# Dummy matmuls and two short reads in the first microseconds of a fused linear-attention and MLP kernel

## The chip, the cores and the metric

The kernel runs on one core of one Trainium2 chip. The time is the device time of one execution in microseconds; the one used core is also the slowest core. Profiles come from the hardware profiler, taken in one execution of the program; their times are counted from the first instruction of the program's span.

## What is computed

The first part is a linear attention with 8 batches, 8 heads, 576 positions and 64 features per head. Its feature map is a ReLU whose output is weighted by a cosine and by a sine of the position. The second part is an MLP over the resulting 4608 rows of 512 features, with a hidden width of 2048 and a Swish whose slope `beta` differs per hidden feature.

```python
def phi(x, c, s):
    r = np.maximum(x, 0.0)
    return np.concatenate([r * c, r * s], axis=-1)
k_p, q_p = phi(k, cos_w, sin_w), phi(q, cos_w, sin_w)
kv = np.einsum('bhsf,bhsd->bhfd', k_p, v)
z = np.sum(k_p, axis=2)
num = np.einsum('bhsf,bhfd->bhsd', q_p, kv)
den = np.einsum('bhsf,bhf->bhs', q_p, z)[..., None] + 1e-06
x = (num / den), heads side by side            # 4608 x 512
h = x @ w_in                                   # 512 x 2048
g = h / (1 + exp(-beta * h))
out = g @ w_out                                # 2048 x 512
```

## The kernel before

The 4608 rows are worked in nine chunks of 512 rows (`TCH`). Each chunk goes through `x @ w_in` into PSUM, a Swish on ScalarE, and `g @ w_out`; from the second chunk on, TensorE uses sums of blocks of the operands (tiles `S1` to `S4`, `T1` to `T4`), made on VectorE, to save matmuls. The attention of batch b runs ahead of the chunk that needs it. The order of the work is written out by hand: every engine executes its instructions in the order of the code, and only semaphores hold an engine back.

What matters here is the opening, before the first chunk. The steps, with the lines of the profile:

- SyncE issues the loads of batch 0 in the order q (two halves), v first half, k first half, v second half, k second half (two pieces), and then `w_in`, all with `load_raw` (L79) and `load_w` (L103). They lie in one hardware queue. ScalarE issues a small load of `beta` (L131).
- GpSimd makes the position numbers `it9` (L142) and two identity matrices: `identf` (64 by 64, float32, L162) and `ident` (128 by 128, bfloat16, L164). It multiplies part of v by the sine (`v_scale`, L209) once v is there.
- VectorE clears `zeros`, which is a part of `S1` (L145 and L160), and makes `tan9` from sine and cosine (L175, L176). Later it copies the tangent table from PSUM (L694), takes the ReLU of q (`q_relu`, L193), multiplies the transposed q by the tangent (`tan_mul`, L223), multiplies v by the cosine (`v_scale`, L209) and takes the ReLU of a part of k (`k_relu`, L193).
- TensorE first executes `warm_pe(58, 48)` (L685): 58 matmuls of zeros by zeros with 48 columns, whose result nobody reads. Then it transposes the tangent (L689) and `beta` (L692), executes 6 dummies of 128 columns and 9 of 48 (L700, L701), transposes q with `ident` in two groups of nine (`q_turn_pe`, L235) with one dummy of 512 columns between them (L704), executes `warm_long(2)` (float32 dummies on raw q, L679), and goes on with `kv_mm` (L276) and `num_mm` (L297). All bfloat16 dummies stand at L675 in the profile.
- The division (L308, L312, L319), the transposes of x (L356) and the first matmuls of chunk 0 (L386) follow.

`S2` is a constant tile of bfloat16, 128 partitions by 8 by 256. In the kernel before, it is written for the first time by the sums of the second chunk (L406).

The 58 copies out of `o_sb` that GpSimd issues (L537) go through its own, software-made queue.

Of the kernel before, what the change touches and what calls it, by code (L numbers as in the profile page):

```python
# [10 lines left out]
FP32 = mybir.dt.float32  # L11
# [5 lines left out]
P = 128  # L17
NQ = 9
# [4 lines left out]
def kernel(  # L23
# [14 lines left out]
    nc = tc.nc  # L38
# [21 lines left out]
    part = ctx.enter_context(tc.tile_pool(name="part", bufs=2))  # L60
# [29 lines left out]
    S1, S2, S3, S4 = (const.tile([P, JT // 2, TCH // 2], BF16, name=f"S{i}") for i in (1, 2, 3, 4))  # L90
# [69 lines left out]
    nc.vector.memset(zeros[:, P:512], 0.0)  # L160
    identf = const.tile([HP, HP], FP32, name="identf")
    make_identity(nc, identf)  # L162
    ident = const.tile([P, P], BF16, name="ident")
    make_identity(nc, ident)  # L164

# [29 lines left out]
    def q_relu(b, jp, eng="dve", n0=0, n1=NQ):  # L195
        return relu(qb[:, jp, n0:n1].rearrange("q n (j d) -> q j n d", j=2),
                    raw_tile(b, "q")[:, 2 * jp : 2 * jp + 2, n0:n1], eng)
# [29 lines left out]
    def q_turn_pe(b, jp, bank, hold=False):  # L227

        parts = ((0, 0, 5), (1, 5, NQ))
        v2 = []  # L230
        for i, n0, n1 in parts:
            t = ps[:, bank + i].bitcast(BF16)[:, 0 : (n1 - n0) * P].rearrange("q (n c) -> q n c", c=P)
            v2.append(t)
            for n in range(n0, n1):
                nc.tensor.matmul(t[:, n - n0, :], lhsT=qb[:, jp, n, :], rhs=ident,  # L235
                                 is_transpose=True, start=(n == n0), stop=(n == n1 - 1))
        def take(e, i):
            _, n0, n1 = parts[i]
            if e == "act":
                nc.scalar.copy(qts[b % 2][:, jp, n0:n1], v2[i])  # L240
            else:
                tan_mul(nc.vector, qs_first[:, jp, n0:n1], v2[i], n0, n1)

        if hold:
            return take
        for e, i in (("act", 0), ("dve", 1), ("act", 1), ("dve", 0)):
            take(e, i)
# [425 lines left out]
    def warm_pe(count, w=512, bank=1):  # L673
        for i in range(count):
            nc.tensor.matmul(ps[:, bank, 0:w], lhsT=zeros[:, 0:P], rhs=zeros[:, 0:w], start=True, stop=True)  # L675
# [6 lines left out]
    beta = const.tile([P, JT], FP32, name="beta")  # L682
    rbeta = const.tile([P, JT], FP32, name="rbeta")

    warm_pe(58, 48)  # L685

    for bank, n0, n1 in ((6, 0, 5), (7, 5, NQ)):
        for n in range(n0, n1):
# [8 lines left out]
    nc.vector.tensor_copy(ps[:, 0, 0:NQ], cos9)  # L697
    nc.vector.tensor_copy(ps[:, 0, 16 : 16 + NQ], sin9)
    q_relu(0, 1)
    warm_pe(6, 128, bank=2)  # L700
    warm_pe(9, 48, bank=2)  # L701
    q_turn_pe(0, 0, 4)
    nc.vector.reciprocal(rbeta, beta)
    warm_pe(1)  # L704
# [387 lines left out]
```

## Time and profile before

| What | us |
| --- | --- |
| Three runs: median (lowest to highest) | 273.6 (273.07 to 273.94) |
| Span of the profiled execution, first to last instruction | 272.7 |
| TensorE busy in the span | 265.3 (97%) |
| VectorE busy | 224.0 (82%) |
| ScalarE busy | 188.4 (69%) |
| GpSimd busy | 68.3 (25%) |

No time of its own beside the span is given for the profiled execution. The runs are 0.4 to 1.2 us above its span, the median 0.9 us: what lies around the span, and the differences between executions.

In the rows of the profile, "PE" is TensorE's matmul, "PEld" its weight load, "DVE" VectorE, "ACT" ScalarE, "POOL" GpSimd and "SP" SyncE; a "q" behind a name is the engine's instruction queue, which issues DMAs. [...] A row of the windows gives busy time of each engine in a stretch, the clock that TensorE was granted, the share of time that the 16 DMA engines were busy, and the bytes that they moved per second.

### The profile page before, as it was taken

To read this page: it belongs to the slowest core of one execution; us is meant where nothing else is said; L and a number is where in the kernel's file an instruction comes from. 1 tells how busy PE (TensorE), PEld (TensorE's weight loads), DVE (VectorE), ACT (ScalarE), POOL (GpSimd) and SP (SyncE) were. 2 spreads that over 40 slices of the span, in tenths; PEclk is the share of its full clock that TensorE was granted. 3 is DMA by queue.
4 is the path that set the end of the run, shared out by engine and by line. 5 is a ranking of instruction groups with operands and counts; after the bars stand their busy time and mean duration, and the time that the engine had idled before them with its cause. 6 is when DMAs were issued, how large, how long until landed. Compare 5 with 4: busy or idle time off the path is not lost.

```text
span 272.7 us, 8970 instructions
## 1 busy us (share of the span) xinstructions
PE 265.3 (97%) x3712; PEld 206.8 (76%) x3712; DVE 224.0 (82%) x596; ACT 188.4 (69%) x384; POOL 68.3 (25%) x89
## 2 busy tenths in 40 slices
PE   8899999999899999999999999999999999999994
PEld 8554455455784588888888888888888888888883
DVE  5989969499989889789989997899589768757852
ACT  4778777796419656899489966996696179428920
POOL 1444000510078000660085009300840060000001
PEclk9999999999999999999999999999999999999999
DMA  6999999999969999994589439943600570015005
GB/s 237 374 395 383 392 390 319 379 201 336 284 130 311 240 348 226 240 313 103 147 216 370 92 58 223 332 71 62 181 2 2 61 185 1 2 27 130 0 2 155
DMA packets 50681, 54.00 MB, mean 198 GB/s; under 512 B 31232, under 2 KB 31760, under 8 KB 50640
## 3 DMA queue, kind: packets, MB, share of 16 engines
q1 hardware_dynamic: 47504, 45.55, 59.1%
q0 software_dynamic: 2784, 7.61, 9.6%
q8 instruction: 29, 0.48, 0.7%
q10 hardware_dynamic: 352, 0.27, 0.4%
q14 instruction: 12, 0.10, 0.1%
HBM read 36.71 MB, written 9.44 MB: 169 GB/s over the span
## 4 chain that ended last, share of the span: by engine, by line
PE 85%; DVE 9%; DMA 3%; SPq 1%; issue 1%; ACT 1%; DVEq 0%
PE ps L621 32%; PE ps L511 27%; PE ps L386 10%; PE ps L544 5%; PE ps L563 4%; PE ps L297 3%; DMA raw_v<-in_v_dram 3%; PE ps L276 3%; DVE vb L219 1%; DVE xs L319 1%; DVE qs L223 1%; SPq L79 1%; DVE S L406 1%; DVE rk L193 1%; DVE qb L193 0%
## 5 line engine op out<-in xcount | busy, mean ns | idle before, releaser
L537 POOL DMA_DIRECT2D out_dram<-o_sb x58 | 33.9, 591 | 147.3 <-ACT o_sb L658 86.3
L420 ACT ACTIVATE g_t<-ps,beta 128x512 bf16<-128x512 f32 x96 | 60.3, 702 | 1.4 <-PE ps L511 1.3
L621 PEld LDWEIGHTS <-S 128*128 128x128 bf16 x448 | 43.4, 98 | 5.2
L511 PE MATMUL ps<-w_stage 128*128 128x256 bf16 x288 | 46.6, 272 | 0.1
L386 PE MATMUL ps<-xt,win 128*128 128x512 bf16 (+1 forms) x196 | 42.8, 375 | 0.1
L511 PEld LDWEIGHTS <-w_stage 128*128 128x128 bf16 x384 | 37.3, 98 | 5.1 <-issue 0.2
L487 DVE TENSOR_TENSOR ps<-ps,p 128x256 f32<-128x256 f32 x74 | 30.5, 428 | 8.6 <-PE ps L511 3.0
L394 ACT ACTIVATE g_t<-ps,beta 128x512 bf16<-128x512 f32 x48 | 32.3, 688 | 7.2 <-PE ps L386 7.1
L621 PEld LDWEIGHTS <-g_t 128*128 128x128 bf16 x336 | 32.3, 98 | 4.5 <-ACT g_t L420 0.4
L386 PEld LDWEIGHTS <-win 128*128 128x128 bf16 x196 | 18.7, 98 | 21.1 <-issue 0.5
L511 PE MATMUL ps<-xt,win 128*128 128x256 bf16 x192 | 32.9, 273 | 0.0
L511 PEld LDWEIGHTS <-win 128*128 128x128 bf16 x288 | 28.0, 98 | 3.4
L621 PE MATMUL ps<-wout,g_t 128*128 128x256 bf16 x224 | 28.9, 273 | 0.0
L406 DVE TENSOR_TENSOR S<-g_t 128x512 bf16<-128x512 bf16 (+1 forms) x66 | 25.7, 418 | 3.3 <-ACT g_t L420 1.7
L480 ACT COPY ps<-ps 128x256 f32<-128x256 f32 x62 | 22.6, 383 | 7.5 <-PE ps L621 4.0
L217 ACT ACTIVATE vb<-raw_v,sin 128x256 bf16<-128x256 f32 (+1 forms) x58 | 26.0, 503 | 1.5 <-DMA raw_v<-in_v_dram 1.5
L621 PE MATMUL ps<-T,S 128*128 128x256 bf16 x224 | 26.6, 273 | 0.0
L621 PE MATMUL ps<-wout,S 128*128 128x256 bf16 x224 | 26.4, 273 | 0.0
L319 DVE TENSOR_TENSOR xs<-ps,rden 128x768 bf16<-128x768 f32 (+4 forms) x26 | 22.8, 884 | 0.9 <-DVE rden L312 0.2
L223 POOL TENSOR_TENSOR qs<-qt,tanr 128x1152 bf16<-128x1152 bf16 x6 | 14.3, 2387 | 27.4 <-PE ps L563 21.0
L658 ACT COPY o_sb<-ps 128x512 f32<-128x512 f32 x11 | 6.3, 587 | 20.1 <-PE ps L621 20.1
L487 DVE TENSOR_TENSOR ps<-ps,u 128x256 f32<-128x256 f32 x36 | 15.3, 427 | 5.3 <-PE ps L511 3.3
(112 smaller groups left out, 414.7 us busy)
## 6 DMA issues: line engine op xcount, KB each, us to landing
raw_v<-in_v_dram SPq DMA_DIRECT2D x7, 1152.0 KB, 9.7
raw_k<-in_k_dram SPq DMA_DIRECT2D x7, 1152.0 KB, 9.5
raw_q<-in_q_dram SPq DMA_DIRECT2D x7, 1152.0 KB, 7.4
out_dram<-o_sb POOLq DMA_DIRECT2D x58, 128.0 KB, 4.5
w_stage<-in_moe_w_in_dram SPq DMA_DIRECT2D x3, 1024.0 KB, 12.8
w_stage<-in_moe_w_out_dram SPq DMA_DIRECT2D x2, 1024.0 KB, 7.9
w_stage<-in_moe_w_out_dram SPq DMA_DIRECT2D x4, 512.0 KB, 11.9
out_dram<-o_sb SPq DMA_DIRECT2D x10, 128.0 KB, 2.4
```

The lines of the kernel that those rows point to most:

```text
L217: got = nc.scalar.activation(o, a, AF.Copy, scale=t[:, n : n + 1])
L223: return eng.tensor_tensor(dst.rearrange("q n (g p) -> q n g p", g=2), src.rearrange("q n (g p) -> q n g p", g=2), tanr[:, n0:n1].unsqueez ...
L319: nc.vector.tensor_tensor(o.rearrange("q j n s d -> q j (n s) d"), nv[:, :, a:z, :, 0:D].rearrange("q j n s d -> q j (n s) d"), rden[:, :, ...
L386: nc.tensor.matmul(ps[:, h_bank(c, jt), i * 64 : (i + w) * 64], lhsT=win[jt // 4][:, mi, (jt % 4) * P : (jt % 4 + 1) * P], rhs=xt[:, i : i ...
L394: return nc.scalar.activation(gs[c, jt // 4][:, jt % 4], ps[:, h_bank(c, jt)], AF.Silu, scale=beta[:, jt : jt + 1])
L406: return nc.vector.tensor_tensor(o, l, r, op=op)
L420: return nc.scalar.activation(gs[c, jt // 4][:, jt % 4], bank, AF.Silu, scale=beta[:, jt : jt + 1])
L480: return nc.scalar.copy(at("a", 0), at("b", 0))
L487: nc.vector.tensor_tensor(dst, at("b", 0), st["p5"], op=ALU.add)
L511: nc.tensor.matmul(dst, lhsT=l[:, g], rhs=r[:, :, g * HP : (g + 1) * HP], start=start and g == 0, stop=g == 1, skip_group_check=True)
L537: (eng or own).dma_start(out=out_v[bb, n][:, m0:m1], in_=o_sb[hf * HP : (hf + 1) * HP, m0:m1])
L621: nc.tensor.matmul(dst, lhsT=l(i), rhs=r[:, i], start=start and i == 0, stop=i == order[-1], skip_group_check=True)
```

## The change

In the opening, `warm_pe(58, 48)` becomes `warm_pe(5)`, that is 5 dummies of 512 columns; the 6 of 128 columns and 9 of 48 become 2 of 512 and 2 of 48. The other dummies stay. Counted over TensorE's instructions, 64 matmuls and 64 weight loads are gone, of some 7,400 instructions.

Between the making of `identf` and of `ident`, GpSimd issues two DMAs. Each reads from batch 0 of v, or of k, 16 floats (64 bytes) at each of 64 places: 16 destination partitions (every eighth of the partition order that `load_raw` uses) by 4 groups of heads. They land in `S2`, where nothing reads them. The real loads of v and k are unchanged, as are the orders on VectorE, ScalarE and SyncE.

```diff
     identf = const.tile([HP, HP], FP32, name="identf")
     make_identity(nc, identf)
+
+    def early_rows(src, part):
+        rows = src[0].rearrange("(j g) (p n) d -> (g p) j (n d)", g=2, n=NQ)[0:P:8, :, 0:16]
+        nc.gpsimd.dma_start(out=part, in_=rows)
+
+    first = S2.rearrange("q i t -> q (i t)").bitcast(FP32)[0:P:8].rearrange("q (i j e) -> q i j e", j=4, e=16)
+    early_rows(v, first[:, 0])
+    early_rows(k, first[:, 1])
     ident = const.tile([P, P], BF16, name="ident")
     make_identity(nc, ident)
...
-    warm_pe(58, 48)
+    warm_pe(5)
...
     q_relu(0, 1)
-    warm_pe(6, 128, bank=2)
-    warm_pe(9, 48, bank=2)
+    warm_pe(2, bank=2)
+    warm_pe(2, 48, bank=2)
     q_turn_pe(0, 0, 4)
```

## The prediction

> **What bounds the kernel now.** I read the busy times first, then the chain of waits over the first 20 us, VectorE's timeline and the windows there, and last the durations of equal matmuls before and after 9 us.
>
> ```profile
> PE 265.3 (97%) x3712; PEld 206.8 (76%) x3712; DVE 224.0 (82%) x596; ACT 188.4 (69%) x384; POOL 68.3 (25%) x89
> 18.60:30.00 11.40, 11.35 (x74) 5.58 (x75) 10.34 (x23) 9.51 (x15) 2.94 (x5) 1.00 1.04 387
> ```
>
> TensorE fills the span, and from 18.6 us on it is busy without a break (11.35 of 11.40 us). So a microsecond won or lost by 18.6 us is won or lost at the end. The change acts before that, where TensorE's 97% says nothing, since its work there is largely dummies.
>
> ```profile
> 3.16 9.06 DMA raw_v<-in_v_dram
> 12.25 0.92 DVE vb L209
> 18.65 0.40 PE ps L356 x4
> ```
>
> The chain there starts with the second half of v, issued at 3.16 and landed at 12.22, and then runs through VectorE (12.25 to 18.60) until TensorE's transposes of x at 18.65. The chain names a DMA, but the reader should ask how long VectorE would have been busy without it:
>
> ```profile
> 5.13 0.75 DVE L193 TENSOR_SCALAR qb<-raw_q 128x1152 bf16<-128x1152 f32 x1
> 6.32 0.76 DVE L193 TENSOR_SCALAR qb<-raw_q 128x1152 bf16<-128x1152 f32 x1
> 9.16 1.34 DVE L209 TENSOR_TENSOR vb<-raw_v,ps 128x1152 bf16<-128x1152 f32 x1
> 10.46 0.86 DVE L193 TENSOR_SCALAR rk<-raw_k 128x512 bf16<-128x512 f32 x1
> 11.24 0.81 DVE L223 TENSOR_TENSOR qs<-ps,tanr 128x640 bf16<-128x640 bf16 x1
> 12.25 1.35 DVE L209 TENSOR_TENSOR vb<-raw_v,ps 128x1152 bf16<-128x1152 f32 x1 [0.19 <-DMA raw_v<-in_v_dram]
> ```
>
> VectorE waits for v only 0.19 us (12.05 to 12.25). Before that, its only idle stretch from 5.13 us is about 0.07 us ahead of the ReLU of q's second half, which landed at 6.30. From 6.32 its instructions touch each other. The data arrive only just in time, but VectorE's own work is as long.
>
> ```profile
> 4.00:5.00 1.00, 1.00 (x11) 0.84 (x10) 0.64 (x2) 0.58 (x2) 0.00 (x0) 1.00 1.04 406
> 5.00:6.00 1.00, 1.00 (x16) 1.00 (x17) 1.00 (x4) 0.00 (x0) 0.00 (x0) 1.00 0.95 311
> 6.00:7.00 1.00, 1.00 (x13) 0.92 (x10) 0.89 (x3) 0.31 (x1) 0.00 (x0) 1.00 1.02 350
> 7.00:8.00 1.00, 1.00 (x9) 0.80 (x8) 0.96 (x3) 0.54 (x2) 0.00 (x0) 1.00 1.00 350
> 8.00:9.00 1.00, 1.00 (x6) 0.71 (x4) 1.00 (x3) 1.00 (x2) 0.00 (x0) 1.00 1.03 373
> ```
>
> The last two numbers are the busy share of the DMA engines and GB/s. When v and k begin to move, at 5 us, the engines stay busy but move less: against 406 GB/s, the four stretches lack 95, 56, 56 and 33 KB, 240 KB in all, or 0.59 us of the full rate. The packet records show why: most packets of 2304 bytes take 0.093 us, but the first of v, at 5.12 us, took 0.96 us, and some 70 up to 9.7 us took 0.13 to 0.75 us.
>
> ```profile
> L235 PE MATMUL ps<-ident,qb x18: 289/314/314, 5.9 to 8.2; 128*128 128x128 bf16 x18
> L356 PE MATMUL ps<-ident,xs x16: 219/219/229, 15.2 to 18.8; 128*128 128x128 bf16 x16
> L679 PE MATMUL ps<-raw_q,S x6: 592/592/1017, 8.3 to 13.6; 128*128 128x512 f32 x6
> ```
>
> Equal transposes took 314 ns up to 8.2 us and 219 ns after 15 us (minimum/median/maximum stand in the rows), and the float32 dummy 1017 ns at 8.26 and 592 ns from 9.1 on. TensorE thus ran slowly until 9.0 us, where the clock's record begins with 1.0; the windows' 1.00 before that is only its absence. It had been busy since 0.99 us.
>
> **The change part by part.** *First dummies.* Before: 58 in 2.50 us (0.99 to 3.49), starts 0.040 us apart. After: 5 of 512 columns. The one such dummy at 6.88 us let its successor start at 7.30, so 0.43 us each, 2.13 us; they need all of `zeros`, cleared at 1.16, and end near 3.35. The tangent's transposes wait for `tan9`, ready at 3.42. They start at 3.56 as before: cost 0. The margin is 0.1 to 0.2 us; without it VectorE's table copies at 4.36 and all behind them come later by what is missing, less the 0.07 us of idle ahead of 6.32.
>
> *Second dummies.* Before 15 from 4.90 to 5.94; after 2 x 0.43 + 2 x 0.04 = 0.93 us, to 5.83. The transposes of q wait for the ReLU, which ends at 5.88. Cost 0, hidden by the ReLU.
>
> *Clock.* The trace has the old pattern open the clock at 9.0 us and cannot show the new one. One bound: it opens several microseconds earlier. Then 18 transposes go at less than 0.107 us each (5.94 to 6.88 and 7.30 to 8.26), but VectorE, busy from 6.32 on, would gain at most the 0.04 us ahead of 7.12. Other bound: it opens after the first 36 `kv_mm`. The four float32 dummies then stand 0.85 us apart (8.26 to 9.11) and not 0.43, end at 11.7, and `kv_mm` (11.25, 0.70 us long) ends near 12.9 in place of 11.95; ScalarE's copy of kv (12.01) comes 0.9 us later, with its four v products, its ReLU of k (to 14.43) and the second `kv_mm` behind it, which had 0.14 us of room: +0.75 us. I take 0, the value nearest to the row: more columns per weight load is hardly less activity.
>
> [...]
>
> *GpSimd.* Two issues ahead of `ident`. GpSimd's issues of stores have a mean of 0.591 us: 1.2 us, so `ident` is ready at 3.4 in place of 2.16; first use 5.94. Cost 0 with 2.5 us of cover; without it, each microsecond would delay q's transposes. GpSimd's next work is v at 9.14. Its first stores come at 50.81, and no order there changes. `S2` is next written at 67.9, far behind the landing.
>
> *Early reads.* Issued at 1.6 and 2.2 us. Nearest rows for landing: 2.6 us for the 8 KB of `beta`, 4.5 us for 128 KB stores of GpSimd. So v's places are touched by 4.2 to 6.1 us and k's 0.6 us later; v's real packets start at 5.0, k's near 6.5. Gain, if the touches take all the slow packets away: v's second half lands 0.59 us earlier. VectorE can use only 0.19 of it, and 0.04 elsewhere: -0.23 us. If they take nothing away: 0. Cost: 128 short packets on 16 engines, 8 each. `beta`'s 512-byte packets took 0.025 us, so 0.2 us; this lies in front of q's second half, whose landing VectorE follows within 0.02 us. The other bound is a slow first packet per engine there (second rival). I take the gain at 0.23, since a third of the slow packets gone already gives the 0.19, and the cost at 0.05, between 0 and 0.2: q's half lands with its slowest engine, and most of the others, done up to some 0.8 us earlier in the packet records, have room for eight short packets.
>
> *Sum.* 0 + 0 + 0 - 0.23 + 0.05, about -0.2 us: span 272.5, and with the 0.9 us that the median lies above the span, 273.4. I say 273.3, as some executions may also open the clock earlier.
>
> **The rivals.** *The clock was the matter in other executions* (faster). The runs spread over 0.87 us, which is about the +0.75 us of a late opening. If the executions at 273.60 and 273.94 paid for it and wide dummies always open the clock in time, the new time is the lowest run less the sum: 273.07 - 0.2 to 0.4, 272.7. For it: clock open only after 8 us of dummies, so it is near the point (10.4 us, where the float32 dummies end) from which it costs. Against: only one execution is traced, and its span is itself within 0.4 us of the lowest run.
>
> *Slow first packets moved in front of q* (slower). If the places are slow because they are new to an engine, the early read pays this itself, at 3 to 5 us, on the engines that carry q. With the 0.96 us packet there, q's second half lands at 7.2, all of VectorE comes 0.9 us later, the wait of 0.19 vanishes, and 0.2 us of short packets join: +0.9 us, 274.5. It decides once q is more than 0.2 us late. For it: VectorE's 0.02 us margin at 6.32. Against: 64-byte reads can wait beside q's packets.
>
> [...]
>
> *The reads change nothing* (they come too late, or the slow packets have another cause): 273.6.
>
> **How the numbers follow.** Forecast 0.46 at 273.3, clock 0.32 at 272.7, moved packets 0.14 at 274.5, nothing 0.08 at 273.6. A difference under 0.3% (0.82 us, about the spread of the runs) can't be told from none: faster means under 272.78, slower over 274.42. Faster: most of the second and a tail of the first, 0.34; slower: the third, 0.14; same 0.52. The range goes from 272.4 (full gain and early clock) to 274.4 (most of the moved packets).
>
> **What would show it.** In the new profile: the tangent's transposes still at 3.56 and q's at 5.94; `ident` made by 4 us; windows from 5 to 9 us near 400 GB/s if the touches work; q's ReLU still at 6.32, else the second rival; float32 dummies all at 592 ns if the clock opened earlier; VectorE without the 0.19 us wait and L356 at 18.45. The forecast falls if L356 moves by more than 0.5 us, or if it stays and the end moves.

## The result, and the profile after

The changed kernel is slower: 278.7 us, median of six runs (277.03 to 279.55), against 273.85 us (273.07 to 274.86) for the kernel before in six. The ratio is 1.0162, with a 95% interval of 1.0141 to 1.0184. The traced execution after took 277.81 us with a span of 276.0, so 1.8 us lie around the span. By that, the traced execution of before (span 272.7) was one of about 274.5 us, 0.65 above the median. The two traces therefore show 3.3 of the 4.85 us between the medians. One run of the reads alone (277.71 us) and one of 16 dummies more (278.66 us), in the experiments below, were slow at a lower clock (0.994 and 0.988), are untraced, and stay out of the medians and ratios.

The totals hardly help. These lines of the page after are the engines' busy times, the granted clock in 40 slices of 6.9 us, and the queue that carries instructions.

```profile
PE 265.9 (96%) x3648; PEld 204.6 (74%) x3648; DVE 223.8 (81%) x596; ACT 188.2 (68%) x384; POOL 68.4 (25%) x91
PEclk9989999999999999999999999999999999999999
q8 instruction: 28, 0.46, 0.7%
```

TensorE is as busy as before, and the 64 matmuls and 64 weight loads are gone. One slice of the clock shows an 8. The last row stood at `q8 instruction: 29, 0.48, 0.7%` in the page of before, a row that is easy to pass over at 0.7%. The packet records say what it is: 29 packets of 16 KB before, 28 after.

VectorE's timeline after (start, duration, engine, line, operation; in brackets the idle time ahead of it and what ended it) shows where its part of the forecast went.

```profile
6.23 0.76 DVE L201 TENSOR_SCALAR qb<-raw_q 128x1152 bf16<-128x1152 f32 x1
...
11.66 1.35 DVE L217 TENSOR_TENSOR vb<-raw_v,ps 128x1152 bf16<-128x1152 f32 x1
...
15.07 1.17 DVE L115 CAST win<-w_stage 64x512 bf16<-64x512 f32 x2
18.90 0.17 DVE L316 TENSOR_TENSOR den<-ps,eps 128x14 f32<-128x14 f32 x1 [2.65 <-PE ps L305]
```

q's ReLU is at 6.23 (6.32 before), and v's second half at 11.66 (12.25 before) without a wait for a DMA. The opening did gain. Then VectorE sits idle for 2.65 us, waiting for TensorE. So the next view is the chain of waits between 10 and 30 us (start, duration, what).

```profile
15.10 0.40 PE ps L364 x4
15.50 0.41 PE ps L305 x30
15.90 2.42 issue
18.32 0.65 PE ps L305 x30
18.97 2.63 PE ps L394 x6
```

The transposes of x (L364, L356 before) start their second group at 15.10; before, it was 15.68. Then, between two halves of a row of `num_mm` (L305), comes 2.42 us of "issue": the profile knows of nothing that TensorE waited for. TensorE's own timeline has the place.

```profile
15.67 0.21 PE L305 MATMUL ps<-kv,qs 64*64 64x65 bf16 x4
15.70 0.20 PE L305 MATMUL ps<-kv,qt 64*64 64x65 bf16 x2
18.32 0.26 PE L305 MATMUL ps<-kv,qt 64*64 64x65 bf16 x2 [2.42 <-issue]
...
105.41 0.83 PE L629 MATMUL ps<-T,S 128*128 128x256 bf16 x6 [0.99 <-issue]
```

A group of four equal matmuls is torn in two: two run at 15.70, the other two 2.6 us later, with the same operands long at hand. (Rows of neighbouring matmuls overlap: the first two above start 0.03 us apart and show 0.21 and 0.20 us.) In the trace of before the same group is whole:

```profile
16.29 0.20 PE L297 MATMUL ps<-kv,qt 64*64 64x65 bf16 x4
```

The hole ends with no semaphore, so the description of the kernel, by which only semaphores hold an engine back, leaves something out. A second such hole stands at 104.42. The windows after (busy time of PE, PEld, DVE, ACT, POOL with their counts, granted clock, DMA share, GB/s) show what surrounds the first.

```profile
15.00:18.30 3.30, 0.86 (x40) 0.59 (x38) 1.18 (x3) 1.67 (x4) 2.82 (x5) 0.96 1.05 395
18.30:22.00 3.70, 3.68 (x45) 1.94 (x46) 2.96 (x10) 0.66 (x3) 0.00 (x1) 0.58 1.04 386
```

The DMA engines are full (1.05) through the hole. Near its end the granted clock falls: the clock's record has 0.5 from 18.02 to 21.43. The first six matmuls of `x @ w_in` took 2.63 us there (18.97 in the chain above); in the trace of before the same six are the row `16.81 1.46 PE L386 MATMUL ps<-xt,win 128*128 128x512 bf16 x6`. That is 1.17 us more.

**The account of the traces.** Opening earlier: -0.58 us. First hole: +2.42. Half clock on six matmuls: +1.17. Second hole: +0.99. One wait of before at 69.19, of 0.96 us and on semaphores, is absent: -0.96. Sum +3.04 of the 3.3; some 0.3 us I did not trace.

**What the hole is.** Queue 8 carried 29 packets of 16 KB for TensorE's 7,424 matmuls and weight loads, about 256 instructions to a packet. The division is only rough (28 packets for 7,296 after); the places of the holes are exact. I number TensorE's records, that is its matmuls, weight loads and waits, in order of their start. In the changed kernel and the experiments 17 holes of 0.5 us or more behind 13 us have no wait. Ten of them end at record 450, or 450 and a multiple of 256 (706, 1986, 2754, 3010, 3778, 5314); the other seven, all behind number 1200, end two to four numbers short of such a place, and I take it that those traces lack some records. The first packet after began at 15.91, and TensorE went on at 18.32, 2.4 us later. My reading: instructions come in blocks by DMA, beside the data (the page gives queue 8 0.7% of the 16 engines' span), and the block that TensorE needed at record 450 was late, so that it had no instructions. Before, 128 more instructions stood ahead, so the same boundary lay among other work. The experiments test that.

### The profile page after: what moved, and what is told of

It reads as the page before. It is cut to its first block, busy times and chain, and to the rows that moved or that the text cites. A ratio compares the mean times of both kernels' runs of the same rounds, so it can differ in the third digit from the quotient of the medians.

```text
span 276.0 us, 8847 instructions
## 1 busy us (share of the span) xinstructions
PE 265.9 (96%) x3648; PEld 204.6 (74%) x3648; DVE 223.8 (81%) x596; ACT 188.2 (68%) x384; POOL 68.4 (25%) x91
## 4 chain that ended last, share of the span: by engine, by line
PE 88%; DVE 9%; issue 2%; ACT 1%; DVEq 0%
PE ps L629 31%; PE ps L519 27%; PE ps L394 11%; PE ps L552 5%; PE ps L305 4%; PE ps L284 3%; PE ps L571 3%; DVE qs L231 2%; DVE S L414 1%; DVE vb L227 1%; PE ps L683 1%; DVE xs L327 1%; PE ps L243 1%; PE ps L364 1%; DVE qb L201 0%
## 5 line engine op out<-in xcount | busy, mean ns | idle before, releaser
L545 POOL DMA_DIRECT2D out_dram<-o_sb x58 | 32.6, 570 | 151.9 <-ACT o_sb L666 86.4
L394 PE MATMUL ps<-xt,win 128*128 128x512 bf16 (+1 forms) x196 | 44.3, 383 | 0.0
L227 DVE TENSOR_SCALAR vb<-raw_v,cos 128x256 bf16<-128x256 f32 x63 | 20.0, 367 | 0.0
```

The lines of the kernel that those rows point to most:

```text
L227: got = nc.vector.tensor_scalar(o, a, scalar1=t[:, n : n + 1], scalar2=None, op0=ALU.mult)
L394: nc.tensor.matmul(ps[:, h_bank(c, jt), i * 64 : (i + w) * 64], lhsT=win[jt // 4][:, mi, (jt % 4) * P : (jt % 4 + 1) * P], rhs=xt[:, i : i ...
L545: (eng or own).dma_start(out=out_v[bb, n][:, m0:m1], in_=o_sb[hf * HP : (hf + 1) * HP, m0:m1])
```

## The experiments

The ratios are to the kernel before, run on the same chip, with 95% intervals.

**Only the dummies, only the reads.** The first takes the change's three edits of `warm_pe` without the DMAs, the second the two DMAs without those edits.

```diff
-    warm_pe(58, 48)
+    warm_pe(5)
...
-    warm_pe(6, 128, bank=2)
-    warm_pe(9, 48, bank=2)
+    warm_pe(2, bank=2)
+    warm_pe(2, 48, bank=2)
```

> The nine wide dummies in place of 73 narrow ones, without the two early reads. Theory (TensorE's instructions come in blocks over the DMA engines; 128 fewer instructions ahead of the dense small matmuls let TensorE use up its block before the next one has come): a hole of about 2.4 us in TensorE inside the second half of the num matmuls (L297) near 16 us, that waits for no semaphore, the first 16 KB instruction packet after 15 us, and a time of 277 to 279.5 us. Rival 1 (the early reads cause the loss): no hole, 273 to 274.2 us. Rival 2 (wide dummies upset the clock gate, and the hole is a consequence): clock lost before any hole.

> The kernel before with the two early reads added, all 73 narrow dummies kept. Theory: no hole near 16 us, first 16 KB instruction packet near 10 us as before, 273.2 to 274.2 us (ratio 0.997 to 1.002). Rival 1 (the reads cause the loss): 277 us or more.

The dummies alone: 278.72 us (four runs), ratio 1.0174 (1.0121 to 1.0227). The reads alone: 273.84 us (nine runs), 1.0003 (0.9977 to 1.0029). So the whole loss is the dummies'. TensorE's timeline with the dummies alone has the hole at the same record:

```profile
15.97 0.20 PE L297 MATMUL ps<-kv,qt 64*64 64x65 bf16 x2
18.92 0.22 PE L297 MATMUL ps<-kv,qt 64*64 64x65 bf16 x2 [2.75 <-issue]
```

A later block is late in this trace too, with a hole of 1.13 us that ends at 106.88. The four runs also bound what the clock adds: the two at a mean clock of 1.0 took 277.42 and 278.04, the two at 0.992 and 0.994 took 279.4 and 280.15, about 2 us more.

**The count restored.** Wide dummies and reads as in the change, but 66 dummies of 16 columns added and two wide ones taken away, so that TensorE's count is that of before.

```diff
-    warm_pe(5)
+    warm_pe(3)
+    warm_pe(32, 16)
...
     warm_long(2)
+    warm_pe(34, 16)
```

> The changed kernel with TensorE's instruction count restored: 3 wide dummies and 32 of 16 columns at the start, 34 of 16 columns after the float32 dummies, so that as many instructions as before precede the kv matmuls. Reads kept. Theory: the hole near 16 us is gone, 273 to 274.5 us. Rivals (reads, or wide dummies and the clock): still 277 us or more, or a clock lost near 16 to 18 us.

Measured 273.69 us (ten runs), 0.9993 (0.9974 to 1.0011). The timeline at the same matmuls, no group torn:

```profile
16.34 0.23 PE L305 MATMUL ps<-kv,qt 64*64 64x65 bf16 x4
...
16.81 0.21 PE L305 MATMUL ps<-kv,qt 64*64 64x65 bf16 x4
16.84 0.21 PE L305 MATMUL ps<-kv,qs 64*64 64x65 bf16 x4
```

Sixty-four more matmuls that compute nothing bring 5 us back. The kind of dummy isn't the matter; their number is. Record 450 now lies in the second `kv_mm`, and a break of 0.18 us stands exactly there in the records (15.10 to 15.28, merged in the view): the block came just in time.

**64 dummies more.** If only the place in blocks of 256 matters, 128 instructions more should hurt like 128 fewer.

```diff
-    warm_pe(58, 48)
+    warm_pe(90, 24)
...
     warm_long(2)
+    warm_pe(32, 16)
```

> The kernel before with 64 dummies more (90 of 24 columns in place of 58 of 48; 32 of 16 columns after the float32 dummies), no early reads, no wide dummies: the count is shifted by +128 instructions, which is the same place in a block of 256 as -128. Theory: a hole inside the second half of the num matmuls as in the changed kernel, 1.5 to 3 us, and 276 to 280 us. Rivals (fewer instructions as such, the wide dummies, the reads): no hole, 273.5 to 275 us, the rise only from a later start of the kv matmuls.

Measured 279.61 us (four runs), 1.0208 (1.017 to 1.0247), with the hole one block later in the count (at record 706) but at the same instructions:

```profile
16.08 0.20 PE L297 MATMUL ps<-kv,qt 64*64 64x65 bf16 x2
18.57 0.22 PE L297 MATMUL ps<-kv,qt 64*64 64x65 bf16 x2 [2.30 <-issue]
```

Two later holes stand in this trace as well, 0.93 us to 105.46 and 1.25 us to 131.03. Together with the last one, this experiment rules out that too little or too weak dummy work is the cause.

**The opening's DMA load taken away.** The changed kernel, with all loads of `w_in` held until ScalarE's second copy of kv; one run.

```diff
-            nc.sync.dma_start(out=st[:, a : a + step], in_=w_in_v[:, a : a + step, i * 512 : (i + 1) * 512])
+            got = nc.sync.dma_start(out=st[:, a : a + step], in_=w_in_v[:, a : a + step, i * 512 : (i + 1) * 512])
+            if behind is not None:
+                after(got, behind, "w_in behind kv")
...
-    load_w("in", 0, 2)
...
-    for i in range(1, 4):
-        load_w("in", i)
...
-    kv_take((1,), 6, eng="act")
+    held = kv_take((1,), 6, eng="act")
+    load_w("in", 0, 2, held)
+    for i in range(1, 4):
+        load_w("in", i, 4, held)
```

> The changed kernel with all loads of w_in held until ScalarE has copied the second kv (about 15 us), so that the DMA engines have little to carry between 13 and 15.5 us; TensorE's instructions are the same. The h matmuls then wait for w_in, and the time is longer for that (about 277 to 282 us). Theory with the DMA load as the cause of the late block: the first 16 KB packet runs by 14 us and there is no hole without a semaphore in the second num matmuls. Rival (a block always takes about 6 us): the packet near 16 us and the hole of about 2.4 us stay.

It took 282.7 us, a little over the 277 to 282 expected. TensorE now waits 4.05 us for `w_in`, and two later blocks are late (1.71 us to 54.39, 1.38 us to 110.29); that time says nothing of the hole in the opening. The two DMA views from 12 us on (queue, packets, MB, share of the 16 engines), first of the changed kernel, 12 to 15.5 us, then of this one:

```profile
q1 hardware_dynamic: 670, 1.30, 101.9%
```

```profile
q1 hardware_dynamic: 46, 0.09, 6.5%
q8 instruction: 1, 0.02, 2.1%
```

With the engines full, no block came by 15.5. With the engines idle, it came at 13.20, 2.7 us earlier than in the changed kernel, though TensorE reached its 200th record at the same time (12.46 against 12.29). The timeline then passes record 450, at 15.86, without a break:

```profile
15.82 0.21 PE L305 MATMUL ps<-kv,qs 64*64 64x65 bf16 x4
15.86 0.20 PE L305 MATMUL ps<-kv,qt 64*64 64x65 bf16 x4
...
16.08 0.21 PE L305 MATMUL ps<-kv,qs 64*64 64x65 bf16 x4
20.34 0.39 PE L394 MATMUL ps<-xt,win 128*128 128x512 bf16 x1 [4.05 <-POOL win L115]
```

TensorE's instructions are the same in both up to there, so in this pair of traces it is the data moving beside the block that makes it late. It is one pair, and with full engines the delay differs too (see the table further down).

**Other counts.** If the mechanism holds, the count has better and worse values. Each of these is the kernel before with its first dummies changed; the first of the four was run with the early reads too.

```diff
-    warm_pe(58, 48)
+    warm_pe(74, 37)
...
-    warm_pe(58, 48)
+    warm_pe(42, 48)
...
-    warm_pe(58, 48)
+    warm_pe(62, 45)
...
-    warm_pe(58, 48)
+    warm_pe(50, 48)
```

16 dummies more:

> The kernel before with 16 narrow dummies more at the same number of columns (74 of 37 in place of 58 of 48): +32 instructions. Theory: the block boundary moves to before the kv matmuls and the next to behind the second num matmuls, where TensorE uses 256 instructions in 5.9 us or more: no hole or one under 0.5 us, 273.2 to 274.3 us. Rival (any move of the count costs): 275 us or more.

16 more, with the reads:

> 74 narrow dummies of 37 columns and the early reads together. Theory: no hole; the reads bring at most 0.3 us: 273 to 274 us, not to be told from the kernel before. A reader who holds the reads for worth more expects under 272.8 us.

16 fewer:

> The kernel before with 16 narrow dummies fewer (42 in place of 58), nothing else: 32 instructions less ahead of the dense matmuls. Theory (the block is asked for as TensorE comes to about its 200th instruction, in multiples of 256, and takes about 6 us at this load): the 200th instruction is then the first of the kv matmuls near 11.2 us in place of 7.6, the next 256 are used up by 15.5 us, and TensorE stands still for 1.5 to 2.5 us from about there, earlier in the program than in the changed kernel; 275.5 to 279 us. Rival (it takes 64 fewer, or the wide dummies): no hole, 273 to 274.3 us.

4 more:

> The kernel before with 4 narrow dummies more (62 of 45 columns): +8 instructions. Theory: the first block is asked for while TensorE still waits with dummies (near 7 us) and needed after 14.5 us, no boundary of the kernel before becomes tighter: no hole, 273.2 to 274.3 us, and perhaps a little under the kernel before, whose tightest block (2.5 us at 69 us) gains 0.5 us. Rival (every change of the count costs): 275 us or more.

8 fewer:

> The kernel before with 8 narrow dummies fewer (50 of 48 columns): -16 instructions, half of the step that cost 3.4%. Theory: the first block is asked for near 9.2 us and needed near 15 us, 5.7 us later against about 6 us that it takes: a hole of 0 to 0.7 us in the opening; the block at 69 us gets tighter than before, by 0.6 to 0.9 us, which alone may cost up to 1.5 us: 273.8 to 277 us.

| Edit | us (runs) | ratio | holes without a wait, us |
| --- | --- | --- | --- |
| 16 more | 275.54 (9) | 1.0048 (1.0011 to 1.0085) | 0.69 at 44.24; 0.52 at 155.0 |
| 16 more, reads | 275.48 (10) | 1.0056 (1.0029 to 1.0082) | 0.65 at 43.99 |
| 16 fewer | 283.07 (4) | 1.0342 (1.0266 to 1.0418) | 2.14 at 14.92; 1.02 at 46.62; 3.29 at 71.87 |
| 4 more | 273.55 (12) | 0.9998 (0.9981 to 1.0015) | none |
| 8 fewer | 279.03 (4) | 1.0198 (1.0165 to 1.0231) | 0.92 at 69.13; 1.03 at 180.47 |

The two with 16 more and the one with 8 fewer missed what I expected, and the one with 16 fewer cost more than I expected: with 16 more or fewer I had looked at the opening alone, and not at the boundaries of later batches. With 8 fewer I had reckoned with the boundary at 69 us, but not with the one at 180. The three that missed indeed have no hole in the opening. Those show in TensorE's timelines; first 16 more, then 8 fewer:

```profile
44.05 0.19 PE L297 MATMUL ps<-kv,qt 64*64 64x65 bf16 x1
44.94 0.22 PE L297 MATMUL ps<-kv,qt 64*64 64x65 bf16 x3 [0.69 <-issue]
```

```profile
180.25 0.21 PE L297 MATMUL ps<-kv,qt 64*64 64x65 bf16 x1
181.49 0.22 PE L297 MATMUL ps<-kv,qt 64*64 64x65 bf16 x3 [1.03 <-issue]
```

A group of four torn into one and three: again the same kind of place, in the attention of later batches. With 16 fewer, three boundaries hurt; here are its timeline at the first and the third, and its window behind the third (columns as in the windows above).

```profile
14.33 0.59 PE L276 MATMUL ps<-vb,rk 64*64 64x130 bf16 x28
17.06 0.30 PE L276 MATMUL ps<-vb,rk 64*64 64x130 bf16 x6 [2.14 <-issue]
...
75.16 0.26 PE L297 MATMUL ps<-kv,qt 64*64 64x65 bf16 x1 [3.29 <-issue]
```

```profile
74.00:81.00 7.00, 5.84 (x40) 4.10 (x41) 3.50 (x11) 0.74 (x2) 0.00 (x0) 0.51 1.00 134
```

With the 3.29 us hole comes a clock of 0.51 from 74 to 81 us, so I estimate that it costs about twice its length. With the 2.14 us hole none does: TensorE's clock stayed at 1.0 behind it. In the traced executions a clock of 0.5 came with every hole or wait of 2.30 us and more, and lasted 3.41 us, or twice that. The traced execution with 8 fewer kept a clock of 1.0 and took 275.93; its other three, at 0.986 to 0.994, took 278.43 to 280.03. I did not trace those three.

Four more were expected to do no harm, and did none, but they gained nothing either, although the clock opened at 4.54 us in that trace (8.99 before). VectorE's timeline says why:

```profile
12.09 1.35 DVE L209 TENSOR_TENSOR vb<-raw_v,ps 128x1152 bf16<-128x1152 f32 x1 [0.86 <-DMA raw_v<-in_v_dram]
```

VectorE was early and then waited 0.86 us for v's second half.

**When the opening's block is late.** Numbered as above, record 450 is where TensorE needs the block. The table sets its start, and that of record 200, beside the start of the block's packet.

| Kernel | record 200, us | packet starts | record 450 starts | hole there |
| --- | --- | --- | --- | --- |
| before | 7.73 | 9.93 | 14.76 | none |
| 4 more | 6.93 | 9.67 | 14.55 | none |
| 8 fewer | 11.07 | 11.52 | 14.80 | none |
| count restored | 11.59 | 13.00 | 15.28 | 0.18 |
| `w_in` held | 12.46 | 13.20 | 15.86 | none |
| 16 fewer | 11.33 | 14.51 | 17.06 | 2.14 |
| changed kernel | 12.29 | 15.91 | 18.32 | 2.42 |
| dummies only | 12.55 | 16.24 | 18.91 | 2.75 |

Where there is a hole, TensorE resumes 2.3 to 2.7 us behind the packet's start. Where there is none, record 450 came 2.6 us behind it or later. And the packet starts 0.4 to 3.7 us behind record 200 in all of them, which is the ground for taking some record near 200 as the one that asks for the block; the request itself is not recorded, so that is an inference. Record 194, which is 450 less one block, fits more closely: behind it the packet starts 1.5 to 3.7 us later in the eleven traces with full DMA engines (with 8 fewer it is 2.7, since 2.2 us lie between records 194 and 200 there), and 0.8 us later with `w_in` held.

From record 200 to record 450 TensorE took 7.0 us before, in a stretch with dummies and transposes in it, and would have taken 3.6 us after (12.29 to 15.9), in which `kv_mm` and `num_mm` run densely (the chain above has 30 matmuls of L305 in 0.41 us). From record 200 to the end of the hole, 6.0 us went by (12.29 to 18.32). The count restored shows that this stretch is not the whole story: there, too, only 3.7 us lie between records 200 and 450 (11.59 to 15.28), and almost nothing is lost, because the packet started 1.4 us behind record 200 and not 3.6. So in these traces a late block took two things: few microseconds of work until its boundary, and a long delay of the packet. What sets the delay between 1.5 and 3.7 us when the engines are full, no run here shows.

No version ran faster than both kernels: the count restored, the four more and the reads alone all lie within their intervals of the kernel before.

## Why the prediction was wrong

The forecast was 273.3 us, no change; it came out 278.7.

**The step that failed** is "First dummies ... cost 0", and with it the second dummies' "Cost 0, hidden by the ReLU". The cost at their own place was right: the tangent's transposes started at 3.556 (3.56 forecast) and q's at 5.934 (5.94). But I priced the 128 removed instructions only as time where they stood. They also had a place in the instruction stream. The cover that I would have had to name is the 7.0 us between records 200 and 450 in the trace of before; with 128 fewer, the boundary moves to a stretch where only 3.6 us lie between them, and the block took 6.0 us in that trace (3.6 until its packet started, 2.4 from there on). The term is +2.42 us for the first hole, +1.17 for the clock behind it and +0.99 for the next one; none of my rivals had it, and the slower rival had another mechanism. The page of before had the hint: a queue of 29 instruction packets in a kernel of 7,424 TensorE instructions. Why the packet is delayed more in one kernel than in another stays open.

**Clock, 0** (bounds -0.04 and +0.75). At the opening right: after, the clock opened at 7.78 us with wide dummies, and in other traces at 7.20, 10.12 and 10.15 (wide), and at 4.54 and 8.94 to 9.92 (narrow). The width did not decide it (that more columns per weight load are no less activity was my assumption; what opens the clock, no run shows), and that it cost nothing was partly luck: 10.15 is near the 10.4 us from which the prediction let it cost. The rival "the clock was the matter in other executions" finds no support: the execution with 4 more had it open at 4.54 and took 273.26, against 273.12 for the lowest run of the kernel before beside it. The 0.1 us by which the forecast lies below its sum, for executions that open the clock earlier, no run shows: before was traced once, with the clock open at 8.99 us, and the opening at 4.54 gained nothing. What I did not have is the clock of 0.5 from 18.02 to 21.43 us that came with the hole.

**GpSimd, 0.** Right. The two issues took 0.66 and 0.52 us, and `ident` was ready at 3.36 (3.4 forecast, needed at 5.93).

**Early reads, -0.23 and +0.05.** Here the reasons were wrong and the size small. They were to land between 4.2 and 6.1 us for v and 0.6 later for k; they landed at 6.39 and 7.17, behind the first of v's real packets (5.0 us). They moved not as 128 short packets but as 64: 32 of 256 bytes, of which 23 took 0.018 us but five 0.07 to 1.05 us, and 32 of 4 bytes with 0.009 us each. Most slow packets of 2304 bytes stayed: from 5.0 to 9.7 us, 42 took 0.13 us or more after, up to 1.00 us, against 51 before (the prediction's "some 70" was too many). The windows after were to near 400 GB/s:

```profile
5.00:6.00 1.00, 1.00 (x5) 0.39 (x5) 1.00 (x4) 0.00 (x0) 0.00 (x0) 1.00 1.11 326
6.00:7.00 1.00, 1.00 (x11) 0.92 (x10) 0.96 (x3) 0.31 (x1) 0.00 (x0) 1.00 0.87 310
7.00:8.00 1.00, 1.00 (x11) 0.81 (x10) 0.89 (x2) 0.54 (x2) 0.00 (x0) 1.00 1.01 371
8.00:9.00 1.00, 1.00 (x7) 0.52 (x5) 1.00 (x3) 1.00 (x2) 0.18 (x1) 1.00 0.99 339
```

The last column was 311, 350, 350 and 373 before, so the rate did not rise. v's second half landed between 11.61 and 12.45 us in the five traces with reads (mean 11.88) and between 11.79 and 12.79 in the seven without (mean 12.08): 0.20 us in the means, with ranges that overlap. The second group of x's transposes started at 15.10 after, but at 15.43 with the reads alone and 15.36 with the dummies alone, against 15.68 before; how much of the 0.58 us is the reads' I leave open. The time of the reads alone shows no gain. That was the rival that the reads change nothing, and of the forecast's parts it is the one that came true. The rival of slow packets moved in front of q did not happen in the trace after: q's second half landed at 6.21 and its ReLU ran at 6.23, not 0.9 us later. In two other traces with reads it landed at 6.71 and 7.00, but in one without (8 fewer) at 6.95 too, so that lateness need not be the reads'.

**The forecast's own test.** It was to fall if L356 moved by more than 0.5 us. The transposes of 18.65 came at 21.66, 3.0 us later, while those ahead of the hole came 0.58 us earlier: the place of the loss lies between the two.

**Distance from span to time, 0.9 us.** It is 1.8 us (277.81 against 276.0); the 0.9 compared the median with another execution's span.

## What to carry to other kernels

Count the instructions of a dense engine as well as their time. Here 128 instructions fewer, all of dummies, shifted every later block of 256, and the boundary that fell into a dense run of small matmuls while the DMA engines were full (1.05) left TensorE 2.42 us without work; the kernel lost 4.85 us. When the chain of waits says "issue" between two equal instructions of one group, number the engine's instructions there and look at the times of the instruction queue's packets. When such instructions are replaced, keep their number (the count restored: ratio 0.9993), or try a few numbers, and look at all boundaries of the run, not just the next one (8 fewer: none in the opening, 1.03 us at 180).

## What the runs showed of the hardware

- The opening's block of TensorE's instructions came later beside the data traffic: with the same instructions, its 16 KB packet began 3.6 us behind record 200 with full DMA engines (101.9%) and 0.7 us behind it with nearly idle ones (6.5%). In 16 of 17 holes TensorE went on 2.3 to 2.7 us behind the packet's start; in the other, 4.1 us behind a packet that itself took 2.75 us.
- TensorE paid twice for long holes: in the five traces with a hole or wait of 2.30 us or more the clock was then 0.5 for 3.41 us or twice that, and behind 2.14 us it stayed at 1.0. It did not happen each time: one of six runs of the changed kernel and two of four with the dummies alone had a mean clock of 1.0 and were still 3.2 to 4.4 us slower than the kernel before. Those three are untraced.
- The time does not run evenly with the number of dummies: in medians, 64 fewer cost 4.9 us, 16 fewer 9.2, 8 fewer 5.4, 4 more nothing, 16 more 1.7 and 64 more 6.0.
- Reads of 64-byte pieces on GpSimd's queue landed 4.8 and 4.9 us after their issue (1.61 and 2.26 to 6.39 and 7.17) while the DMA engines, with the other queue, were busy for 0.98 of 2.26 to 7.17 us; over the five traces with reads it was 4.7 to 6.1 us.
